# Batch 0 over SyncE's queue as 32-bit words, stores on GpSimd's queue, full-height tiles, transposes behind the loads

## The chip, the core and the metric

The kernel runs on one core of a Trainium2 chip. A core has five engines with a list of instructions each: TensorE (PE, matrix products), VectorE (DVE), ScalarE (ACT), GpSimd (POOL) and SyncE (SP). They work at the same time and meet only at semaphores; each takes its own list strictly in order. Sixteen DMA engines move data between the main memory (HBM) and the on-chip memory (SBUF). Products go to a small memory of eight banks (PSUM), from where ScalarE or VectorE copies them. The metric is device time in microseconds, as the median of several runs: 201.82 before the change (three runs, 201.66 to 203.79).

## The reference

Inputs are q, k and v of shape (8 batches, 8 heads, 576 rows, 64), and three weights. An attention with keys and values pooled over eight rows is followed by a gated feed-forward stage with a short convolution:

```python
k_p = k.reshape(B, H, S // 8, 8, D).mean(axis=3)      # 72 pooled rows a head; v_p alike
scores = scale * q @ k_p.transpose(0, 1, 3, 2)
attn = softmax(scores)
x = (attn @ v_p) -> (B, S, H * D)                     # 576 x 512 a batch
h = relu(x @ w_in)                                    # 512 -> 1024
conv_out = conv_w[0] * h[s-1] + conv_w[1] * h[s] + conv_w[2] * h[s+1]
out = (h * sigmoid(conv_out)) @ w_out                 # 1024 -> 512, float32
```

All inputs and the output are float32; the kernel computes in bfloat16 with float32 sums.

## The kernel before

One launch does all eight batches. Every step is an operation handed to a planner (`Planner`), with its engine, an estimated duration, what it reads and writes, and a rank. `Planner.order` plays these operations against its own table of durations and writes them out; the list of ranks `prio` decides among operations that could start together, and `act` names the evacuations and copies that go to ScalarE rather than VectorE. The compiled program keeps that order on each engine. Where the planner sees TensorE idle in the first 60 us, it puts matmuls of a zero tile (`warm`, L407), called fillers here; nothing reads their result.

For each batch these steps follow one another; those of different batches overlap:

- **Loads** (`load_k` L468 and L472, `load_v` L488 to L500, `load_q` L439 and L445). GpSimd issues all loads, and its DMAs convert float32 to bfloat16 on the way. Batches 0 to 4 bring q with eight rows of a head side by side; `regroup` (L453) brings them into order. Batches 5 to 7 bring q as five tiles of 128 rows.
- **Pooling** (`pool8`, `attn_k`, `attn_v`): three adds on VectorE, L632, L639 and L649 for k or L695 for v. For k four full transposes and one of a tile of 64 rows follow on TensorE (L662, L663), and two copies into `kz` (L669). For v two masked copies `vblk` (L700, L705).
- **q turned** (`attn_q`): in batches 0 to 4 by TensorE against the identity, 32 matmuls (L735) and copies (L744); in batches 5 to 7 by five crossbar transposes in DMA, issued by SyncE (L718).
- **Scores and exponentials** (`attn_s`): five tiles, L767 and, for the rest of four pairs of heads, L769 on a quarter of the columns each; ScalarE takes the exponential (L775).
- **Value products** (`attn_av`): five tiles of six matmuls (L792, L796); the fifth has 64 rows of output. VectorE divides (L805, L809) into `xx`. In batches 0 to 4 TensorE turns `xx` (L829, the fifth tile with 64 rows) and L835 copies it to `xT`; in batches 5 to 7 SyncE's crossbar transposes do it (L822).
- **Feed-forward**: x times w_in (L849 for batch 0, L872 for the others) with relu on ScalarE; the convolution partly on TensorE (L995), mostly on VectorE and ScalarE (L918 to L937); the gate (L945, L1002) and the product gT (L983).
- **Output** (`mm2` L1026): for each pair of batches nine tiles of 128 rows, copies into one of three output buffers (L1049), and five stores issued by SyncE (L1054); the last tile in two halves (L1039, L1044).

GpSimd also makes the identity matrix `ident`, which the transposes and the small constants of the convolution need. In its list the first five loads stand ahead of it.

SyncE's list before the change has one small load, then the five stores of batches 0 and 1, and after that transposes and stores mixed. Each DMA also waits for the landing of the eighth DMA before it on the same queue.

Of the kernel before, what the change touches and what calls it, by code (L numbers as in the profile page):

```python
# [104 lines left out]
}  # L105
# [9 lines left out]
class Planner:  # L115
# [60 lines left out]
    def order(self):  # L176
# [16 lines left out]
        ring = [0.0] * 4  # L193
# [6 lines left out]
        while avail:  # L200
# [68 lines left out]
            if o.dma is not None:  # L269
                n, each = o.dma  # L270
                if e == "SP":
# [37 lines left out]
def kernel(  # L309
# [14 lines left out]
    P = 128  # L324
# [20 lines left out]
    perm4 = st("perm4", [64, 64], BF16)  # L345
# [23 lines left out]
    attnT = [st(f"attnT{i}", [P, NT, S], BF16) for i in range(2)]  # L369
# [78 lines left out]
    def regroup(b, pr):  # L448
        if PARAMS["rg"][b] in "QT" or PARAMS["qd"][b]:
            return  # L450
        for h in range(0, H, 4):
# [5 lines left out]

    def load_k(b, prio):
        m = b % 2
        src = rows(k, b)  # L460
        acc = PARAMS["acc"][b]
# [14 lines left out]
    def load_v(b, prio):  # L476
        m = b % 2
        src = rows(v, b).rearrange("(c z) e -> z c e", z=2 * Sp)
        acc = PARAMS["acc"][b]
# [38 lines left out]
    def consts():  # L518
# [20 lines left out]
        def fn(e):  # L539
            nc.vector.tensor_copy(out=perm4.rearrange("r (p i) -> r p i", i=TP), in_=ident[0:64, 0:64].rearrange("r (i p) -> r p i", p=8))  # L540
# [64 lines left out]

        for m in range(2):
            def fn(e, m=m):
                nc.vector.memset(kz[m], 0.0)
# [549 lines left out]
```

## Time and profile before

| | |
|---|---|
| median of 3 runs | 201.82 us |
| the profiled execution's own time | 200.92 us |
| span of its instructions | 199.1 us |
| TensorE's granted clock | 1.00 |
| first, last matmul | 2.5 us, ends 195.4 us |
| value products of batch 0 begin | 17.1 us |
| feed-forward of batch 0 begins | 21.7 us |
| last load lands | 114.5 us |
| first crossbar transpose issued | 83.5 us |
| HBM read, written | 33.44 MB, 9.44 MB |

All times of instructions are counted from the start of the span. A matmul's duration in the profile includes the depth of the pipeline: full matmuls of 128 columns show some 220 ns and start every 56 ns. So I compare starts. "Idle before" tells how long an engine had nothing to run before an instruction, and what it waited for. The granted clock is 1.00 in every stretch.

### The profile page before, as it was taken

Reading aid. Unit: us, or ns where it says so; the run is one execution under the profiler, and the core shown is the slowest. Engines: PE = TensorE matmul, PEld = TensorE weight load, DVE = VectorE, ACT = ScalarE, POOL = GpSimd, SP = SyncE. Lnnn points to the kernel's source line nnn. Section 1 sums busy time; section 2 is a strip of 40 time slices with the busy share of each in tenths; the row PEclk is TensorE's granted clock in tenths of the full one; section 3 lists DMA queues with packets and bytes.
Section 4 is the critical chain, followed back from the end, with each engine's and each line's share of the span. In section 5 each row is a group of like instructions: output and inputs, shape, how many; then the busy total and the mean of one; then the engine's idle time right before and its main releaser. Section 6 shows DMA issues by size and latency. Waiting matters only on the chain.

```text
span 199.1 us, 4491 instructions
## 1 busy us (share of the span) xinstructions
PE 190.8 (96%) x1737; PEld 128.9 (65%) x1737; DVE 171.0 (86%) x400; ACT 167.0 (84%) x282; POOL 47.5 (24%) x76
## 2 busy tenths in 40 slices
PE   5999999999999999999999999989999999999992
PEld 5888777777546576767756656547666565765541
DVE  3777999999999999999999999988889997755631
ACT  0677699999995499999999999995999999998410
POOL 7966431543233262761140000000000000000000
PEclk9999999999999999999999999999999999999999
DMA  3999999999999999999999966477112144502324
GB/s 39 185 185 200 204 204 193 207 206 200 195 204 250 268 217 207 159 217 121 113 116 117 70 211 161 85 189 188 28 35 83 65 129 87 211 3 77 135 106 158
DMA packets 52857, 30.00 MB, mean 151 GB/s; under 512 B 33484, under 2 KB 48356, under 8 KB 52836
## 3 DMA queue, kind: packets, MB, share of 16 engines
q0 software_dynamic: 32912, 16.73, 68.1%
q1 hardware_dynamic: 19924, 12.99, 26.9%
q8 instruction: 13, 0.21, 0.4%
q14 instruction: 8, 0.07, 0.1%
HBM read 33.44 MB, written 9.44 MB: 215 GB/s over the span
## 4 chain that ended last, share of the span: by engine, by line
PE 88%; DVE 7%; POOL 2%; DMA 1%; issue 1%; ACT 0%; POOLq 0%
PE psfB L1026 31%; PE psfA L872 25%; PE psfA L792 4%; PE psfA L767 4%; PE psfA L995 4%; PE pswA L407 3%; PE psbB L735 2%; PE psfB L849 2%; DVE xx L809 2%; PE psfA L849 2%; PE psfA L796 2%; PE psbB L829 1%; PE pswB L407 1%; PE psbA L829 1%; DMA xT<-xx 1%; PE psfA L769 1%
## 5 line engine op out<-in xcount | busy, mean ns | idle before, releaser
L1026 PE MATMUL psfB<-w_out,gT 128*128 128x512 bf16 (+1 forms) x282 | 65.5, 378 | 0.0
L872 PE MATMUL psfA<-xT,w_in 128*128 128x288 bf16 x448 | 59.2, 286 | 0.9 <-DMA xT<-xx 0.7
L872 PEld LDWEIGHTS <-w_in 128*128 128x128 bf16 x448 | 42.8, 98 | 14.8 <-issue 1.2
L1026 PEld LDWEIGHTS <-gT 128*128 128x128 bf16 x290 | 27.2, 98 | 29.0 <-issue 0.2
L878 ACT ACTIVATE hT<-psfA 128x576 bf16<-128x576 f32 x56 | 35.2, 651 | 2.2 <-PE psfA L872 2.0
L918 ACT ACTIVATE cv<-hT,cr 128x576 bf16<-128x576 bf16 x37 | 28.3, 779 | 0.2
L809 DVE TENSOR_TENSOR xx<-psfA,rr 128x512 bf16<-128x512 f32 (+1 forms) x40 | 26.8, 683 | 0.9 <-DMA xT<-xx 0.7
L920 DVE TENSOR_SCALAR cv<-hT,cr 128x576 bf16<-128x576 bf16 x71 | 23.9, 363 | 3.9 <-ACT tg L945 2.3
L775 ACT ACTIVATE attnT<-psfA 128x576 bf16<-128x576 f32 x40 | 25.1, 674 | 0.3 <-PE psfA L767 0.2
L983 DVE TENSOR_TENSOR gT<-tg,hT 128x1152 bf16<-128x1152 bf16 x32 | 23.7, 750 | 1.2 <-ACT tg L1002 0.8
L927 DVE TENSOR_TENSOR cv<-cv,hT 128x1152 bf16<-128x1152 bf16 (+1 forms) x31 | 20.8, 672 | 4.0 <-ACT cv L918 3.9
L945 ACT ACTIVATE tg<-cv,cn 128x576 bf16<-128x576 bf16 x31 | 23.2, 775 | 0.9 <-DVE cv L937 0.6
L937 DVE TENSOR_TENSOR cv<-cv 128x1152 bf16<-128x1152 bf16 (+1 forms) x31 | 20.8, 673 | 0.2
L1049 ACT COPY osb<-psfB 128x512 f32<-128x512 f32 x24 | 14.3, 595 | 7.4 <-PE psfB L1026 7.3
L945 ACT ACTIVATE tg<-cv,cs 128x576 bf16<-128x576 bf16 x23 | 17.5, 797 | 0.0
L792 PE MATMUL psfA<-vblk,attnT 128*128 128x130 bf16 (+1 forms) x160 | 15.7, 222 | 0.2
L407 PEld LDWEIGHTS <-zero 128*128 128x128 bf16 x206 | 13.0, 105 | 3.4 <-DVE zero L520 2.5
L792 PEld LDWEIGHTS <-attnT 128*128 128x128 bf16 (+1 forms) x160 | 11.0, 100 | 4.1 <-issue 1.8
L407 PE MATMUL pswA<-zero 128*128 128x128 bf16 x148 | 10.5, 236 | 2.5 <-DVE zero L520 2.5
L767 PE MATMUL psfA<-qT,kz 128*128 128x512 bf16 x64 | 12.3, 286 | 0.4 <-ACT attnT L775 0.4
L439 POOL DMA_DIRECT2D q<-in_q_dram x10 | 8.6, 863 | 12.1 <-DMA k_b<-in_k_dram 4.0
L796 PE MATMUL psfA<-vblk,attnT 128*128 128x130 bf16 (+1 forms) x80 | 11.2, 221 | 0.0
(94 smaller groups left out, 247.8 us busy)
## 6 DMA issues: line engine op xcount, KB each, us to landing
out_dram<-osb SPq DMA_DIRECT2D x14, 512.0 KB, 3.0
k_b<-in_k_dram POOLq DMA_DIRECT2D x8, 512.0 KB, 14.8
v_b<-in_v_dram POOLq DMA_DIRECT2D x7, 512.0 KB, 16.7
q_b<-in_q_dram POOLq DMA_DIRECT2D x4, 576.0 KB, 17.6
out_dram<-osb SPq DMA_DIRECT2D x7, 256.0 KB, 2.1
w_in<-in_moe_w_in_dram POOLq DMA_DIRECT2D x2, 512.0 KB, 11.4
w_out<-in_moe_w_out_dram POOLq DMA_DIRECT2D x2, 512.0 KB, 15.0
q<-in_q_dram POOLq DMA_DIRECT2D x8, 128.0 KB, 12.6
```

The lines of the kernel that those rows point to most:

```text
L407: nc.tensor.matmul(out=t, lhsT=zero[:, 0:P], rhs=zero[:, 0:P], start=True, stop=True)
L775: nc.scalar.activation(out=attnT[m][:, t, :], in_=slot(key).rearrange("p i x -> p (i x)")[:, 0:S], func=ACT.Exp, scale=1.0 / 64.0)
L792: nc.tensor.matmul(out=a[0:n, g, c * w:(c + 2) * w], lhsT=attnT[m][:, s, u0:u0 + n], rhs=vblk[m][:, 2 * s:2 * s + 2, :].rearrange("p x d - ...
L809: nc.vector.tensor_tensor(out=xx[i3][0:n].rearrange("p (g h e) -> p g h e", g=2, h=4), in0=av_view()[:, :, :, 0:D], in1=rr[i3][0:n].rearra ...
L872: nc.tensor.matmul(out=t[:, i, 0:HC], lhsT=w_in[:, c, f * P:(f + 1) * P], rhs=xT[m][:, c, i * HC:(i + 1) * HC], start=(c == 0), stop=(c == ...
L878: nc.scalar.activation(out=h_(b)[:, f, hs(b), 2:S + 2].rearrange("p (i x) -> p i x", i=2), in_=slot(key)[:, :, 0:HC], func=ACT.Relu)
L918: nc.scalar.activation(out=cv[y][:, kk // 2, z0:z1, :], in_=src, func=ACT.Copy, scale=sc)
L920: nc.vector.tensor_scalar(out=cv[y][:, kk // 2, z0:z1, :], in0=src, scalar1=sc, scalar2=None, op0=OP.mult)
L927: nc.vector.tensor_tensor(out=cv[y][:, 0, 0:n, :], in0=cv[y][:, 0, 0:n, :], in1=h_at(2), op=OP.add)
L945: nc.scalar.activation(out=tg[i3][:, zs[z0]:zs[z0] + z1 - z0, :], in_=cv[y][:, 0, z0:z1, :], func=ACT.Tanh if half else ACT.Sigmoid, scale ...
L983: nc.vector.tensor_tensor(out=o_, in0=tg[i3], in1=h2, op=OP.mult)
L1026: nc.tensor.matmul(out=a[:, 0, j0:j1], lhsT=g[:, c, t * P:(t + 1) * P], rhs=w_out[:, c, j0:j1], start=(c == 0), stop=(c == n_fb - 1), skip ...
```

## The change

Five things change together.

1. **Batch 0's q, k and v** come by SyncE's queue as float32, without conversion, into memory that gT uses later (`ks`, `ws`, `qs`): q in four pieces, k in two, v in six, twelve issues beside the one small load. The first adds of the pooling then read float32, and q is regrouped in four copies instead of two.
2. **Stores** of the second and third pair of batches (`sp`) are issued by GpSimd, the others by SyncE.
3. **Full-height tiles**: the fifth k tile is transposed with 128 rows (the upper 64 are zeros), the fifth value tile computes 128 rows of output (the exponentials have 64 more columns for that, set to zero once), and the fifth turn of `xx` is a matmul over 128 rows against a matrix whose lower rows are zeros.
4. **Transposes held** (`xw`): for the planner every crossbar transpose depends on all loads that GpSimd issues. That moves them in the written order; the program gets no wait from it.
5. **The order drawn anew**: new ranks `prio`, a new choice `act`, and new terms in the planner's table: its load queue counts as busy to 12.9 us, and early DMAs of SyncE get their own rule.

In the compiled order GpSimd first makes the identity and the masks' start, then issues q of batch 1, a piece of k of batch 1, half of w_in, k of batch 1, the other half of w_in and v of batch 1. The crossbar transposes stand behind the last store of pair 0 on SyncE, and the stores of pairs 1 and 2 stand behind all loads on GpSimd. There are 224 fillers, where there were 206.

```diff
-    "xw": 0,
+    "xw": 1,
+    "kh": 2,
+    "sp": [0, 1, 1, 0],
...
-        ring = [0.0] * 4
+        ring = [12.9 if PARAMS["kh"] == 2 else 0.0] * 4
...
-                if e == "SP":
+                if e == "SP" and s < 9.0 and o.lat is not None:
+                    o.done = s + d + 2.03
+                elif e == "SP" and s < 9.0:
+                    hring = max(hring, s + d + 0.5, 3.9) + n * each
+                    o.done = hring + self.DMA_LAT
+                elif e == "SP":
...
-    perm4 = st("perm4", [64, 64], BF16)
+    perm4 = st("perm4", [P, 64], BF16)
...
-    attnT = [st(f"attnT{i}", [P, NT, S], BF16) for i in range(2)]
+    attnF = [st(f"attnT{i}", [P, NT * S + 64], BF16) for i in range(2)]
+    attnT = [a[:, 0:NT * S].rearrange("p (t s) -> p t s", t=NT) for a in attnF]
...
+        if b == 0 and PARAMS["kh"] == 2:
+            for x in range(2):
+                for y, (r0, r1) in enumerate(((0, 64), (64, PR))):
+                    def fn(e, x=x, r0=r0, r1=r1):
+                        nc.sync.dma_start(out=qs[x][r0:r1].rearrange("p h i d -> p h (i d)"), in_=rows_q(b)[r0:r1, 4 * x:4 * x + 4])
+                    pl.add(f"ldq0.{x}.{y}", "SP", 0.43, fn, writes=[("qs", x, y)], prio=prio + 0.01 * x, dma=(2 if y else 16, 0.085))
+            return
...
+        if b == 0 and PARAMS["kh"] == 2:
+            for h in range(0, H, 2):
+                def fn(e, h=h):
+                    copy_on(e)(out=q2[0][0:PR, :, h:h + 2, :], in_=qs[h // 4][0:PR, h % 4:h % 4 + 2].rearrange("p h i d -> p i h d"))
+                pl.add(f"qg.{b}.{h}", {"DVE": 1.15, "ACT": 1.04}, 0, fn, reads=[("qs", h // 4, 0), ("qs", h // 4, 1)],
...
+    def early(i, lo, hi):
+        return gT[i].rearrange("p f s -> p (f s)")[:, lo:hi].bitcast(FP32)
+    ks = early(1, 0, NT * 1024).rearrange("p (t e) -> p t e", t=NT)
+    ws = early(0, 0, NT * 1024).rearrange("p (t e) -> p t e", t=NT)
+    qs = [early(i, NT * 1024, NT * 1024 + 4096).rearrange("p (h i d) -> p h i d", i=TP, d=D) for i in range(2)]
...
+        if b == 0 and PARAMS["kh"]:
+            def fn(e):
+                nc.sync.dma_start(out=ks[:, 0:4], in_=src[0:512].rearrange("(t p) e -> p t e", p=P))
+            pl.add("ldk0.0", "SP", 0.43, fn, writes=[("ks", 0)], prio=prio, dma=(32, 0.085))
...
+        if b == 0 and PARAMS["kh"] == 2:
+            for c in range(4):
+                def fn(e, c=c):
+                    nc.sync.dma_start(out=ws[32 * c + 16:32 * c + 32, 4], in_=src[P:P + 16, c])
...
+            for x in range(2):
+                def fn(e, x=x):
+                    nc.sync.dma_start(out=ws[:, 2 * x:2 * x + 2], in_=src[0:P, 2 * x:2 * x + 2])
...
-            nc.tensor.transpose(out=t[:, 0, 512:576], in_=ksum[0:64, 4].rearrange("p i d -> p (i d)"), identity=ident[0:64, 0:64])
+            nc.tensor.transpose(out=t[:, 0, 512:640], in_=ksum[:, 4].rearrange("p i d -> p (i d)"), identity=ident)
...
-                nc.tensor.matmul(out=a[0:n, g, c * w:(c + 2) * w], lhsT=attnT[m][:, s, u0:u0 + n],
+                nc.tensor.matmul(out=a[:, g, c * w:(c + 2) * w], lhsT=attnF[m][:, s * S + u0:s * S + u0 + P],
...
+                if last:
+                    nc.tensor.matmul(out=a[:, 0, c * n:(c + 1) * n], lhsT=xx[i3][:, c * P:(c + 1) * P], rhs=ident[:, 0:n] if tr else perm4, start=c == 0, stop=c == n_dc - 1, skip_group_check=True)
+                    continue
...
-            nc.sync.dma_start(out=out_rows[r:r + n * P, :].rearrange("(i p) d -> p i d", p=P), in_=osb[i3][:, 0:n, :])
-        pl.add(f"st.{pair}.{tiles[0]}", "SP", 0.4, fn, reads=[("osb", i3, x) for x in range(n)], prio=pr, dma=packets(n * P, 2048, False))
+            (nc.gpsimd if PARAMS["sp"][pair] else nc.sync).dma_start(out=out_rows[r:r + n * P, :].rearrange("(i p) d -> p i d", p=P), in_=osb[i3][:, 0:n, :])
+        pl.add(f"st.{pair}.{tiles[0]}", "POOL" if PARAMS["sp"][pair] else "SP", 0.8 if PARAMS["sp"][pair] else 0.4, fn, reads=[("osb", i3, x) for x in range(n)], prio=pr, dma=packets(n * P, 2048, False))
```

More of the change, by code (lines that the diff above doesn't have):

```diff
@@ L450, in regroup @@
             return
+        if b == 0 and PARAMS["kh"] == 2:
[3 more added lines that the diff above has]
+                pl.add(f"qg.{b}.{h}", {"DVE": 1.15, "ACT": 1.04}, 0, fn, reads=[("qs", h // 4, 0), ("qs", h // 4, 1)],
+                       writes=[("q", 0, h), ("q", 0, h + 1)] + ([("qt", 0)] if h == 6 else []), prio=pr + 0.01 * h,
+                       free=[("qn", "R", 0, t) for t in range(NT)])
+            return
         for h in range(0, H, 4):
@@ L460, in load_k, with fn @@
         src = rows(k, b)
+        if b == 0 and PARAMS["kh"]:
+            def fn(e):
+                nc.sync.dma_start(out=ks[:, 0:4], in_=src[0:512].rearrange("(t p) e -> p t e", p=P))
+            pl.add("ldk0.0", "SP", 0.43, fn, writes=[("ks", 0)], prio=prio, dma=(32, 0.085))
+            def fn(e):
+                nc.sync.dma_start(out=ks[0:64, 4], in_=src[512:576])
+            pl.add("ldk0.t", "SP", 0.43, fn, reads=["kzs"], writes=[("ks", 1)], prio=prio + 0.01, dma=(4, 0.085))
+            return
         acc = PARAMS["acc"][b]
@@ L539, in fn @@
         def fn(e):
-            nc.vector.tensor_copy(out=perm4.rearrange("r (p i) -> r p i", i=TP), in_=ident[0:64, 0:64].rearrange("r (i p) -> r p i", p=8))
+            nc.vector.tensor_copy(out=perm4.rearrange("r (p i) -> r p i", i=TP), in_=ident[:, 0:64].rearrange("r (i p) -> r p i", p=8))
         pl.add("perm1", "DVE", 0.15, fn, reads=["ident"], writes=[("perm", 1)], prio=-47)
@@ L604, in consts, with fn @@
                        writes=[("dw", f, kk)], prio=-3 + 0.5 * f)
+        if PARAMS["kh"]:
+            def fn(e):
+                nc.vector.memset(ks[64:P, 4], 0.0)
+            pl.add("zks", "DVE", 0.4, fn, writes=["kzs"], prio=-75)
+            def fn(e):
+                nc.vector.memset(ws[:, 4], 0.0)
+            pl.add("zvs", "DVE", 0.54, fn, writes=["vzs"], prio=-74)
         for m in range(2):
+            def fn(e, m=m):
+                nc.vector.memset(attnF[m][:, NT * S:], 0.0)
+            pl.add(f"zat{m}", "DVE", 0.08, fn, writes=[("zat", m)], prio=-40 + 35 * m)
             def fn(e, m=m):
@@ L632, in fn @@
                 nc.vector.tensor_tensor(out=p1[:, t0:t1, :], in0=src[m][:, t0:t1, 0:256], in1=src[m][:, t0:t1, 256:512], op=OP.add)
-            rk = rs + ([("kz", m)] if name == "k" else [])
+            st_ = b == 0 and (PARAMS["kh"] if name == "k" else PARAMS["kh"] == 2)
+            rk = rs + ([] if st_ else [("kz", m)] if name == "k" else [])
             if not acc:
-                pl.add(f"{name}p1.{b}.{x}", "DVE", 0.075 + 0.1334 * n, fn, reads=rk, writes=[("p1", y) for y in ys], prio=pr)
+                pl.add(f"{name}p1.{b}.{x}", "DVE", 0.075 + (0.267 if st_ else 0.1334) * n, fn, reads=rk, writes=[("p1", y) for y in ys], prio=pr)
                 rk = [("p1", y) for y in ys]
@@ L644, in attn_k @@
         m = b % 2
-        pool8(b, "k", k_b, pr, ((0, 5, (0, 1), [("k", m, 0), ("k", m, 1)]),))
+        if b == 0 and PARAMS["kh"]:
+            pool8(b, "k", [ks], pr, ((0, 5, (0, 1), [("ks", 0), ("ks", 1), "kzs"]),))
+        else:
+            pool8(b, "k", k_b, pr, ((0, 5, (0, 1), [("k", m, 0), ("k", m, 1)]),))
         def fn(e):
@@ L662, in fn @@
                 nc.tensor.transpose(out=t[:, 0, i * P:(i + 1) * P], in_=ksum[:, i].rearrange("p i d -> p (i d)"), identity=ident)
-            nc.tensor.transpose(out=t[:, 0, 512:576], in_=ksum[0:64, 4].rearrange("p i d -> p (i d)"), identity=ident[0:64, 0:64])
-        pl.add(f"kT.{b}", "PE", 0.29, fn, reads=["ksum", "ident"], writes=[("kTp", b)], prio=pr, take=key, free=[("kz", m, 0), ("kz", m, 1)])
+            nc.tensor.transpose(out=t[:, 0, 512:640], in_=ksum[:, 4].rearrange("p i d -> p (i d)"), identity=ident)
+        pl.add(f"kT.{b}", "PE", 0.31, fn, reads=["ksum", "ident"], writes=[("kTp", b)], prio=pr, take=key, free=[("kz", m, 0), ("kz", m, 1)])
         kzi = [None]
@@ L675, in attn_v, with vkey @@
         m = b % 2
-        tail = [*[("v", m, 2 + c) for c in range(4)]]
-        parts = ((0, 2, (0,), [("v", m, 0)]), (2, 5, (1,), [("v", m, 1)] + tail)) if b == 0 else ((0, 5, (0, 1), [("v", m, 0), ("v", m, 1)] + tail),)
+        vk = "ws" if b == 0 and PARAMS["kh"] == 2 else ("v", m)
+        def vkey(y):
+            return (vk, y) if vk == "ws" else ("v", m, y)
+        tail = [vkey(2 + c) for c in range(4)] + (["vzs"] if vk == "ws" else [])
+        parts = ((0, 2, (0,), [vkey(0)]), (2, 5, (1,), [vkey(1)] + tail)) if b == 0 else ((0, 5, (0, 1), [("v", m, 0), ("v", m, 1)] + tail),)
         if PARAMS["vp"][b]:
@@ L691, in attn_v @@
         else:
-            pool8(b, "v", v_b, pr, parts)
+            pool8(b, "v", [ws] if vk == "ws" else v_b, pr, parts)
             def fn(e):
@@ L770, in fn @@
                                          start=True, stop=True, tile_position=(0, 32 * c))
-        pl.add(f"sc.{b}.{t}", "PE", 0.25 if t < 4 else 0.48, fn, reads=[("kz", m, 0), ("kz", m, 1)] + [("qT", m, g) for g in gs] + [("qA", m)],
+        pl.add(f"sc.{b}.{t}", "PE", 0.25 if t < 4 else 0.37, fn, reads=[("kz", m, 0), ("kz", m, 1)] + [("qT", m, g) for g in gs] + [("qA", m)],
                writes=[("scp", b, t)], prio=pr, take=key, free=[("at", m, t)])
@@ L795, in fn @@
             for g in range(2):
-                nc.tensor.matmul(out=a[0:n, g, 0:4 * w].rearrange("p (c x d) -> p c x d", x=2, d=w)[:, :, 1], lhsT=attnT[m][:, 4, u0:u0 + n],
+                nc.tensor.matmul(out=a[:, g, 0:4 * w].rearrange("p (c x d) -> p c x d", x=2, d=w)[:, :, 1], lhsT=attnF[m][:, 4 * S + u0:4 * S + u0 + P],
                                  rhs=vblk[m][:, 8 + 2 * g:10 + 2 * g, :], start=False, stop=True, skip_group_check=True)
-        avs[0] = pl.add(f"av.{b}.{t}", "PE", 0.35, fn, after=avs[0], reads=[("at", m, s) for s in range(NT)] + [("va", m, 0), ("va", m, 1)],
+        avs[0] = pl.add(f"av.{b}.{t}", "PE", 0.35, fn, after=avs[0], reads=[("at", m, s) for s in range(NT)] + [("va", m, 0), ("va", m, 1), ("zat", m)],
                writes=[("avp", b, t)], prio=pr, take=key, free=[("rr", i3), ("xx", i3)])
@@ L822, in fn @@
                 nc.sync.dma_start(out=xT[m][:, :, u0:u0 + n], in_=xx[i3][0:n, :], transpose=True)
-            pl.add(f"xD.{b}.{t}", "SP", 1.27, fn, reads=[("xx", i3)], writes=[("xT", m, t)], prio=pr + 0.3, dma=(1, 0.65), lat=0.1)
+            pl.add(f"xD.{b}.{t}", "SP", 1.35, fn, reads=[("xx", i3)], writes=[("xT", m, t)], prio=pr + 0.3, dma=(1, 0.65), lat=0.4)
             return
         def fn(e):
-            a = slot(key2, True)
+            a = slot(key2, not last)
             for c in range(n_dc):
-                nc.tensor.transpose(out=a[:, 0, c * P:c * P + n], in_=xx[i3][0:n, c * P:(c + 1) * P], identity=(ident[0:n, 0:n] if tr else perm4 if last else perm))
-        pl.add(f"xt.{b}.{t}", "PE", 0.14 if last else 0.222, fn, reads=[("xx", i3), ("perm", 0), ("perm", 1)], writes=[("xtp", b, t)],
+                if last:
+                    nc.tensor.matmul(out=a[:, 0, c * n:(c + 1) * n], lhsT=xx[i3][:, c * P:(c + 1) * P], rhs=ident[:, 0:n] if tr else perm4, start=c == 0, stop=c == n_dc - 1, skip_group_check=True)
+                    continue
+                nc.tensor.transpose(out=a[:, 0, c * P:c * P + n], in_=xx[i3][0:n, c * P:(c + 1) * P], identity=(ident if tr else perm))
+        pl.add(f"xt.{b}.{t}", "PE", 0.13 if last else 0.222, fn, reads=[("xx", i3), ("perm", 0), ("perm", 1)], writes=[("xtp", b, t)],
                prio=pr + 0.3, take=key2, free=[("xT", m, t)])
@@ L835, in fn @@
             copy_on(e)(out=xT[m][:, :, 128 * t:128 * t + w],
-                       in_=slot(key2)[:, 0, 0:512].rearrange("p (c a) -> p c a", c=4)[:, :, 0:w])
-        pl.add(f"xte.{b}.{t}", {"ACT": 0.48, "DVE": 0.335} if not last else {"ACT": 0.265, "DVE": 0.205}, 0, fn, reads=[("xtp", b, t)], writes=[("xT", m, t)],
+                       in_=slot(key2)[:, 0, 0:4 * w].rearrange("p (c a) -> p c a", c=4))
+        pl.add(f"xte.{b}.{t}", {"ACT": 0.48, "DVE": 0.335} if not last else {"ACT": 0.27, "DVE": 0.33}, 0, fn, reads=[("xtp", b, t)], writes=[("xT", m, t)],
                prio=pr + 0.3, give=key2)
```

3 lines of the change are left out of this document (added), and 97 rows, old and new, of the table PARAMS.

## The prediction

> **What bounds the kernel now.** I read the page first (busy shares and the chain that ended last), then the waits of TensorE, then its timeline around the places where it waited, then the DMA issues and DMA rate by stretch.
>
> ```profile
> span 199.1 us, 4491 instructions
> ...
> PE 190.8 (96%) x1737; PEld 128.9 (65%) x1737; DVE 171.0 (86%) x400; ACT 167.0 (84%) x282; POOL 47.5 (24%) x76
> ...
> PE 88%; DVE 7%; POOL 2%; DMA 1%; issue 1%; ACT 0%; POOLq 0%
> ```
>
> TensorE is the bound, and 88% of the chain that ended last is its own work, not waiting. So the end moves by what TensorE's list gains or loses in work, by the start of its real work, and by the few holes in it. The start, from TensorE's timeline (start us, us, engine, line, operation):
>
> ```profile
> 10.39 0.40 PE L662 MATMUL psbB<-ident,ksum 128*128 128x128 bf16 x4
> ...
> 17.09 0.40 PE L792 MATMUL psfA<-vblk,attnT 128*128 128x130 bf16 x4
> ...
> 21.70 0.82 PE L849 MATMUL psfA<-xT,w_in 128*128 128x384 bf16 x4
> ```
>
> Batch 0's pooled keys are turned at 10.4, its value products begin at 17.1, its first feed-forward product at 21.7 us. Until then TensorE mostly multiplies zeros (L407). The last matmul ends at 195.4. The only hole after that start worth more than 0.5 us, from the same view:
>
> ```profile
> 126.86 0.39 PE L662 MATMUL psbB<-ident,ksum 128*128 128x128 bf16 x4
> 127.18 0.20 PE L663 MATMUL psbB<-ident,ksum 64*128 64x64 bf16 x1
> 127.31 0.66 PE L767 MATMUL psfA<-qT,kz 128*128 128x512 bf16 x4
> ...
> 131.26 0.41 PE L767 MATMUL psfA<-qT,kz 128*128 128x512 bf16 x2 [0.38 <-ACT attnT L775]
> ...
> 134.64 0.28 PE L872 MATMUL psfA<-xT,w_in 128*128 128x288 bf16 x1 [0.57 <-DMA xT<-xx]
> 135.09 1.15 PE L872 MATMUL psfA<-xT,w_in 128*128 128x288 bf16 x8 [0.17 <-DMA xT<-xx]
> ```
>
> Between 130.5 and 135.1 the starts are 2.2 us later than the same shapes need elsewhere (0.57, 0.30, 0.26, 0.74 and 0.33): exponentials of batch 6 and crossbar transposes of batch 5 come late. The first three lines show a second thing. Full matmuls of 128 columns start 0.056 apart; four of them and one of 64 rows should take 0.28, and take 0.45 to the next start. Each step between a full shape and one of at most 64 rows or columns costs about 0.095 us.
>
> Last, the loads (DMA issues with count and median us to landing; then stretches, their last two columns the DMA share and GB/s):
>
> ```profile
> xT<-xx SPq DMA_TRANSPOSE x15, 2.5
> qT<-q SPq DMA_TRANSPOSE x10, 10.8
> ...
> qT<-q_b SPq DMA_TRANSPOSE x5, 2.6
> ...
> 56.00:60.00 4.00, 4.00 (x24) 1.90 (x22) 3.92 (x10) 4.00 (x8) 1.58 (x3) 1.00 1.25 207
> 83.00:104.00 21.00, 20.83 (x195) 14.81 (x194) 20.59 (x51) 20.86 (x35) 7.03 (x10) 1.00 1.68 143
> 104.00:115.00 11.00, 11.00 (x87) 7.04 (x86) 10.40 (x23) 10.87 (x19) 0.64 (x1) 1.00 1.89 95
> ```
>
> Transposes among loads (from 83.5 us) land after 10.8 us instead of 2.6, and the rate falls from 207 to 143 and 95 GB/s. The last load lands at 114.5.
>
> **The change, part by part.**
>
> *Full-height tiles.* Steps removed: kT, 0.172 a batch (0.45 against 5 x 0.056) in 8 batches, 1.4 us; the last value tile, in and out, 0.19 x 8 = 1.5; the last turn of the output in batches 0 to 4, 0.19 x 5 = 0.9. The wider matmuls cost nothing: the turn keeps 64 columns, kT adds 64 columns (0.02, counted). Of the 3.8 us, 3.5 lie behind the first feed-forward matmul, where TensorE is never short of work. The chip's price of a full shape in these places is a row (0.056), so I keep no other bound than 0 and 3.8.
>
> *Order drawn anew.* Fillers on `zero`: 224 against 206; behind the first feed-forward matmul 58 against 27. They hold the place of waits that the new order expects in batch 1, but run whatever comes: 31 x 0.056 = +1.7. Eleven q transposes (0.032 each) and four turns (0.056) now stand ahead of that matmul: -0.6 behind it.
>
> *Batch 0 over SyncE's queue.* Thirteen issues of about 0.43 us (L528's row); SyncE has nothing else until a store at 56.3, so the issuing is free. GpSimd loses nine issues there, so `ident` comes at 2.2 us rather than 5.5, and its first load (q of batch 1) issues at about 2.2 instead of 9.3. Every engine moves 108 packets of 2 KB for batch 0. Trace packets of the load queue pass at 0.08 us an engine at full load, so 8.6 us; the small constant's first packet comes 0.7 us after its issue, so the flow starts at 2.0, and v is complete at 11.3 if SyncE's queue is alone. No row shows a load on this queue. Stores show how two queues meet: the store issued at 56.3 moved its first packet at 60.0, 3.7 us late, and from 65 to 66.5 us the trace has 146 packets of SyncE's queue beside 145 of GpSimd's. If GpSimd's first packets (3.6 us) are held as long, SyncE's queue is alone to 7.3, then at half rate: k complete at 7.6, v at 14.6 (before: 8.4 and 14.7). With no such hold v comes at 18.3. I take the middle, because the same trace shows both the hold and the halves; the ends 11.3 and 18.3 stay for the range.
>
> The f32 adds: nearest rows are the bf16 add of 1280 (0.74 start to start) and f32 from PSUM into xx (0.60 for 512, 1.17 ns an element, so 1.50 for 1280). Source type decides, so +0.76 for k and +0.45 for v's two pieces. They stand ahead of the scores.
>
> When do value products start? Not before TensorE's own list allows. The first ScalarE copy of q must follow its table load (1.28): cw comes at about 4.7 (6.5 now, less the earlier `ident`), three scalings of 0.29 and the copy follow, done about 7.9. Then in order: 16 q transposes, 69 fillers (3.9) to 12.4, 8 q transposes, kT at 12.8, kz, scores from 14.1, the last at 16.2, 26 fillers, value products at about 17.85. From v at 14.6 by the before-distance of 2.4 plus 0.45: 17.45. So 17.85, 0.75 late against 17.09; the first feed-forward matmul follows 4.4 to 4.6 later as now, at 22.3: **+0.6**. Both w_in halves come no later than now, since GpSimd's queue is served from 4 to 7 us on.
>
> *Stores on GpSimd, transposes held.* Pairs 1 and 2 store behind all loads on GpSimd's in-order queue. Pair 1's first store now issues at 114.2 and GpSimd's last load at 104, so nothing waits; if loads ran late, the copies into the three output buffers would, and TensorE's PSUM with them. On SyncE fifteen q transposes follow pair 0's last store, and no store stands between them and the fifteen of xx. Loads without transposes beside them should keep 200 GB/s: 13.4 MB of the 16.7 of this queue have landed by 80 us, the rest takes 17 to 19 us, so 97 to 99 instead of 114.5. "Held" is only an order: the first transpose waits for a tile of q with nine loads still issued behind it. Adding rows along TensorE's list, batch 5's scores stand 91 us after the first feed-forward matmul, at 113; five quiet transposes need 8.5 us (119.3 to 127.8 now). Start by 104 suffices. And 12 us of other work stand between the last values of batch 5 and its feed-forward, where there were 8.6. So most of the 2.2 us hole should go: **-1.5** (bounds 0 and -2.2).
>
> On the transposes, the Trainium skill ("DMA: Bandwidth & Descriptors", Rules for kernel authors) says that a transpose next to ordinary DMAs needs nothing. That is said of data; the 10.8 against 2.6 us above disagree as to time. By it the hole would stay and the sum be 1.5 us worse.
>
> **Sum:** +0.6 - 0.6 - 3.5 + 1.7 - 1.5 = -3.3 us. The profiled execution took 200.9 (span 199.1 and 1.8 around it), so 197.6 (span 195.8). It lay 0.9 under the median of 201.82; the median should become **198.5**.
>
> **The rivals.**
>
> *ScalarE becomes the bound* (0.20). Adding its rows from the first relu on, it reaches batch 1's first relu after 22.0 us (now 16.7), since batch 2's five exponentials now stand before it; TensorE's list gets there after 21.7 (now 18.6). A lead of 1.9 became -0.3; with the first output 0.5 to 0.9 more, and DVE 95% busy beside it, 1 to 1.5 us are lost: 199.8. For it: ACT is over 98% busy from 41 to 60 us. Against: five x 0.67 of cv and two table loads leave it later on.
>
> *Equal shares from the start* (0.15). v at 18.3, value products at 21.15, +3.3 on an in-order engine: 201.8. Against it: the 3.7 us hold. The Trainium skill ("DMA: Bandwidth & Descriptors", SWDGE vs HWDGE vs iDMA) has each DMA engine take turns between the two kinds of queue, which is this rival from the first packet; the 146 beside 145 agree, the late first packet does not.
>
> *Slower: the last loads hold batch 5* (0.12). q tiles are now the very last loads, behind v of batch 7, which waits for batch 5's pooling on a DVE that is 95% busy. TensorE cannot pass its scores. If the last load still lands at 114.5, the transposes end at 123 and the list is 9.7 us late: 208. It decides from about 108 on, where the loss (3.3) eats the gain. For it: loads were slow here; against it: what slowed them has moved.
>
> *It doesn't do what it says* (0.05): padding leaves the steps where they are: 198.5 + 3.5 = 202.
>
> **How the numbers follow.** The forecast, 195 to 199.8, has 0.48. About 1% (199.8 to 203.8) is what a measurement can tell from no change. Faster: 0.48 and half of ScalarE's rival, 0.58. Within 1%: the other half, most of equal shares and of the last rival, 0.27. Slower: the held loads and the tails of the others, 0.15. The range runs down to 195.0: early loads let the start come 0.5 earlier at most, since the fillers stand, the whole hole may go (0.7 more), the profile's 0.9 under the median may not recur, and 1.4 remain for small waits of the old order that the new one lacks. Up to 203.5 it leaves out the held loads and little else.
>
> **What would show it.** In the changed profile: starts 0.056 apart through kT and into the next operation; the first value product near 17.9 and the first feed-forward matmul near 22.3; k and v of batch 0 landing near 8 and 14.6; last load under 100 us; transposes landing in under 3 us but for the first few; no wait over 0.5 us on xT; last matmul near 192. The forecast is wrong if value products begin after 20, if DVE waits for k or v of batch 7, or if TensorE waits for qT.

## The result, and the profile after

The changed kernel takes **216.94 us** (median of four runs, 214.63 to 219.38) where the kernel before takes 202.12 beside it: a ratio of **1.068**, 95% interval 1.056 to 1.079. The forecast was 198.5. One of the four runs of the changed kernel and two of the four of b0_gp_bf16 below were longer at a lower granted clock; the ratio of 1.068 leaves that one out (it is against the mean of the kernel before, 202.42), while the 1.020 of b0_gp_bf16 in the table still contains its two, without which it is 1.011 (204.54 and 205.90 against 203.06). The profiled execution took 217.26 us, its span is 215.6. From its page (span, busy shares, granted clock in tenths over the span, and the chain that ended last by engine):

```profile
span 215.6 us, 4546 instructions
...
PE 192.6 (89%) x1755; PEld 132.3 (61%) x1755; DVE 171.0 (79%) x399; ACT 169.3 (79%) x289; POOL 47.5 (22%) x76
...
PEclk9996699999999999999999999999889999999999
...
PE 57%; ACT 18%; DMA 15%; DVE 6%; SPq 1%; issue 1%; DVEq 0%; ACTq 0%
```

TensorE is busy for about as long as before, but for 89% of the span where it was 96%, and its own work is 57% of the last chain where it was 88%. ScalarE and DMAs have come into that chain, so the time went into waiting. TensorE's timeline in the first 35 us shows the larger part (start us, us, engine, line, operation; in brackets the idle time before and what ended it):

```profile
21.29 0.66 PE L805 MATMUL psbB<-ident,q 72*128 72x72 bf16 x8 [8.17 <-ACT q L470]
...
21.85 0.63 PE L728 MATMUL psbB<-ident,ksum 128*128 128x128 bf16 x4
22.27 0.31 PE L729 MATMUL psbB<-ident,ksum 128*128 128x128 bf16 x1
...
29.63 0.40 PE L862 MATMUL psfA<-vblk,attnT 128*128 128x130 bf16 x4 [1.81 <-DVE vblk L770]
...
34.24 0.81 PE L922 MATMUL psfA<-xT,w_in 128*128 128x384 bf16 x4
```

These answer to the first lines shown of before. The pooled keys are turned at 21.9 (10.4 before), the value products begin at 29.6 (17.1), the first feed-forward product at 34.2 (21.7). TensorE waited 8.2 us for a copy of batch 0's q on ScalarE. ScalarE's own timeline says what that copy waited for:

```profile
20.18 1.99 ACT L470 CAST q<-gT 72x1024 bf16<-72x1024 f32 x2 [9.54 <-DMA gT<-in_q_dram]
```

The loads of batch 0, from the list of DMA issues (queue, count, KB each, median us from issue to landing):

```profile
gT<-in_q_dram SPq DMA_DIRECT2D x2, 512.0 KB, 10.9
gT<-in_k_dram SPq DMA_DIRECT2D x1, 1024.0 KB, 13.2
...
gT<-in_v_dram SPq DMA_DIRECT2D x2, 512.0 KB, 17.5
```

Batch 0's k is complete at 17.0 us (its large piece at 16.2; 7.6 forecast, 8.4 before), the second half of q at 20.1, and v between 22.4 and 26.3 (14.6 forecast). The end of v sets the value products: TensorE then waited for `vblk`, which is made from v, 1.8 us up to 29.6. The second place is where the forecast wanted a hole closed, around batch 5's feed-forward. From TensorE's timeline there:

```profile
142.72 0.39 PE L728 MATMUL psbB<-ident,ksum 128*128 128x128 bf16 x4
142.94 0.22 PE L729 MATMUL psbB<-ident,ksum 128*128 128x128 bf16 x1
143.00 0.65 PE L837 MATMUL psfA<-qT,kz 128*128 128x512 bf16 x4
...
148.34 0.67 PE L837 MATMUL psfA<-qT,kz 128*128 128x512 bf16 x4 [0.63 <-DMA qT<-q_b]
...
151.38 0.28 PE L945 MATMUL psfA<-xT,w_in 128*128 128x288 bf16 x1
154.43 1.83 PE L945 MATMUL psfA<-xT,w_in 128*128 128x288 bf16 x7 [2.77 <-DMA xT<-xx]
```

The hole has grown: 0.6 us without work before batch 7's scores and 2.8 us for batch 5's xT. The seven feed-forward products behind it take 1.83 us, because the granted clock is halved there (last section). But the first three lines show the step that did work. Four turns of the keys and the fifth, now full, take 0.28 us to the next start; before they took 0.45.

For a sum I split TensorE's time from the first feed-forward product to the last matmul in two. Every start-to-start is compared with the median of its shape. An excess of more than 0.23 us, or of more than 0.13 when another engine released the later instruction, is a **wait**; all else is the **list**. All profiled executions, experiments included (us; the ratio is that of the timed runs against the kernel before beside them):

| kernel | first feed-forward | list | waits | last matmul starts | span | ratio (95%) |
|---|---|---|---|---|---|---|
| before | 21.70 | 170.24 | 3.21 | 195.15 | 199.1 | 1 |
| changed | 34.24 | 169.17 | 7.99 | 211.40 | 215.6 | 1.068 (1.056 to 1.079) |
| b0_gp_f32 | 28.30 | 167.64 | 7.75 | 203.69 | 208.9 | 1.037 (1.033 to 1.040) |
| b0_gp_bf16 | 23.42 | 167.48 | 6.52 | 197.41 | 202.8 | 1.020 (1.014 to 1.026) |
| sp_alone | 34.54 | 167.46 | 6.45 | 208.45 | 213.4 | 1.060 (1.055 to 1.064) |
| full_only | 22.37 | 166.76 | 7.18 | 196.31 | 200.2 | 0.989 (0.985 to 0.994) |
| b0_gp_qT3 | 23.44 | 167.47 | 4.35 | 195.25 | 200.0 | 1.000 (0.998 to 1.002) |
| b0_gp_st_sp | 23.74 | 167.56 | 7.43 | 198.74 | 203.9 | 1.010 (1.005 to 1.015) |
| b0_gp_nofill | 23.55 | 164.28 | 9.22 | 197.05 | 202.1 | 1.012 (1.008 to 1.016) |
| full_qT3 | 22.98 | 166.82 | 6.82 | 196.63 | 200.6 | 0.992 (0.989 to 0.996) |
| after_qT3 | 34.52 | 167.49 | 4.18 | 206.18 | 210.3 | 1.045 (1.040 to 1.050) |
| qT3_q3cut | 24.03 | 167.57 | 4.42 | 196.01 | 200.7 | 0.998 (0.995 to 1.001) |

The changed kernel lost 12.5 us at the start, won 1.1 in the list and lost 4.8 in waits; together that is all of the 16.25 us by which its last matmul starts late. Its list contains some 1.7 us of halved clock behind the second hole; the other kernels with the new order and all of its fillers have 167.5 to 167.6.

### The profile page after: what moved, and what is told of

Its sections match the earlier page's. It is cut to its first block, busy times and chain, and to the rows that moved or that the text cites. A ratio compares the mean times of both kernels' runs of the same rounds, so it can differ in the third digit from the quotient of the medians.

```text
span 215.6 us, 4546 instructions
## 1 busy us (share of the span) xinstructions
PE 192.6 (89%) x1755; PEld 132.3 (61%) x1755; DVE 171.0 (79%) x399; ACT 169.3 (79%) x289; POOL 47.5 (22%) x76
## 4 chain that ended last, share of the span: by engine, by line
PE 57%; ACT 18%; DMA 15%; DVE 6%; SPq 1%; issue 1%; DVEq 0%; ACTq 0%
PE psfB L1099 19%; PE psfA L945 19%; DMA gT<-in_k_dram 6%; DMA gT<-in_v_dram 5%; ACT hT L951 4%; ACT tg L1018 4%; PE psfA L1068 3%; ACT cv L991 3%; PE psfA L862 3%; DMA xT<-xx 3%; PE psfA L922 2%; PE psfA L837 2%; DMA qT<-q_b 2%; DVE xx L879 2%; ACT xT L908 2%; ACT attnT L845 2%
## 5 line engine op out<-in xcount | busy, mean ns | idle before, releaser
L945 PE MATMUL psfA<-xT,w_in 128*128 128x288 bf16 x448 | 60.7, 290 | 3.0 <-DMA xT<-xx 2.8
L993 DVE TENSOR_SCALAR cv<-hT,cr 128x576 bf16<-128x576 bf16 x76 | 26.3, 375 | 2.7 <-ACT tg L1018 1.0
L991 ACT ACTIVATE cv<-hT,cr 128x576 bf16<-128x576 bf16 x32 | 24.7, 793 | 0.2
L1018 ACT ACTIVATE tg<-cv,cn 128x576 bf16<-128x576 bf16 x32 | 24.1, 794 | 1.0 <-DVE cv L1010 1.0
L1127 POOL DMA_DIRECT2D out_dram<-osb x10 | 6.8, 684 | 77.6 <-ACT osb L1122 43.8
L416 PEld LDWEIGHTS <-zero 128*128 128x128 bf16 x224 | 15.3, 110 | 3.7 <-DVE zero L569 2.4
L862 PE MATMUL psfA<-vblk,attnT 128*128 128x130 bf16 x160 | 15.7, 223 | 2.1 <-DVE vblk L770 1.8
L862 PEld LDWEIGHTS <-attnT 128*128 128x128 bf16 x160 | 11.8, 99 | 5.9 <-ACT q L477 1.9
L805 PE MATMUL psbB<-ident,q 72*128 72x72 bf16 x140 | 7.0, 204 | 9.2 <-ACT q L470 8.2
L805 PEld LDWEIGHTS <-q 72*128 72x128 bf16 x160 | 6.7, 102 | 10.1 <-ACT q L470 8.3
```

The source lines that it names most:

```text
L862: nc.tensor.matmul(out=a[:, g, c * w:(c + 2) * w], lhsT=attnF[m][:, s * S + u0:s * S + u0 + P], rhs=vblk[m][:, 2 * s:2 * s + 2, :].rearran ...
L945: nc.tensor.matmul(out=t[:, i, 0:HC], lhsT=w_in[:, c, f * P:(f + 1) * P], rhs=xT[m][:, c, i * HC:(i + 1) * HC], start=(c == 0), stop=(c == ...
L991: nc.scalar.activation(out=cv[y][:, kk // 2, z0:z1, :], in_=src, func=ACT.Copy, scale=sc)
L993: nc.vector.tensor_scalar(out=cv[y][:, kk // 2, z0:z1, :], in0=src, scalar1=sc, scalar2=None, op0=OP.mult)
L1018: nc.scalar.activation(out=tg[i3][:, zs[z0]:zs[z0] + z1 - z0, :], in_=cv[y][:, 0, z0:z1, :], func=ACT.Tanh if half else ACT.Sigmoid, scale ...
```

## The experiments

### Where the start went: queue or words

Three kernels keep the changed kernel's orders and move only batch 0's loads. The two on GpSimd's queue issue them ahead of its other loads:

```diff
-  nc.sync.dma_start(out=qs[x][r0:r1]..., in_=rows_q(b)[r0:r1, 4 * x:4 * x + 4])
+  nc.gpsimd.dma_start(out=qs[x][r0:r1]..., in_=rows_q(b)[r0:r1, 4 * x:4 * x + 4])
...
-  for s, e, d, o in pl.order():
+  for s, e, d, o in batch0_loads_and_masks + other_early_loads + rest:   # shortened
```

The second of them also takes the staging buffers as bf16, so that the loads cast:

```diff
-        return gT[i].rearrange("p f s -> p (f s)")[:, lo:hi].bitcast(FP32)
+        return gT[i].rearrange("p f s -> p (f s)")[:, lo // 2:hi // 2]
```

> The changed kernel, with batch 0's twelve loads issued on GpSimd's queue ahead of its other loads; words, adds and all other orders are kept. Theory 'shared start' (the 12.5 us by which the first feed-forward product came late, 34.2 against 21.7, are lost because SyncE's queue got only every second packet from the start, at about 0.097 us a packet): with one queue and batch 0 first, k lands near 8, q's second half near 10.5, v near 14 to 15; first feed-forward product near 23; profile 204 to 206. Rival 'words' (32-bit words are slow to move or to add, on any queue): v still lands after 20, first feed-forward product after 29, profile above 211.

> As b0_gp_f32, but the loads cast to bf16 as before the change. Theory 'shared start': within 1 us of b0_gp_f32 (the adds are 1.2 us shorter in all, not all of it on the path), 203 to 205.5. Rival 'words': this one alone gains, first feed-forward product near 22 and at least 6 us less than b0_gp_f32.

The third leaves batch 0 on SyncE's queue and puts four tiny reads of the landed tiles ahead of GpSimd's first load:

```diff
+  for z, x_ in enumerate((ks[:, 3, 0:1], ws[:, 1, 0:1], ws[:, 3, 0:1], ws[:, 4, 0:1])):
+      nc.gpsimd.affine_select(out=scr[:, z:z + 1], in_=x_, ...)
```

> The changed kernel, with GpSimd's first load held until all of batch 0 has landed over SyncE's queue. Theory 'shared start': alone, SyncE's queue passes a packet in about 0.08 us an engine, so k near 7.5, v near 12 to 13; value products near 18; the first half of w_in, now third on GpSimd's queue from about 13, lands near 24 to 25 and sets the first feed-forward product at 25; profile 206 to 209. Rival 'slow queue' (SyncE's queue needs twice the time for a packet by itself): v still lands after 22, the loads behind it 10 us or more later than in the changed kernel, profile above 222.

Measured, with the moment at which the last piece of v has landed: changed 26.3, sp_alone 20.3, b0_gp_f32 20.3, b0_gp_bf16 16.0 us. The rows of k and v in the lists of DMA issues of sp_alone, b0_gp_f32 and b0_gp_bf16:

```profile
gT<-in_k_dram SPq DMA_DIRECT2D x1, 1024.0 KB, 9.8
gT<-in_v_dram SPq DMA_DIRECT2D x2, 512.0 KB, 12.1
```

```profile
gT<-in_k_dram POOLq DMA_DIRECT2D x1, 1024.0 KB, 7.4
gT<-in_v_dram POOLq DMA_DIRECT2D x2, 512.0 KB, 11.4
```

```profile
gT<-in_k_dram POOLq DMA_DIRECT2D x1, 512.0 KB, 5.8
...
gT<-in_v_dram POOLq DMA_DIRECT2D x2, 256.0 KB, 7.4
```

Each theory had half of it. The queue by itself is not slow: alone, SyncE's brings v as early as GpSimd's does with the same words, both ahead of the 22 of the "slow queue". But words cost 4.3 us of landing on one and the same queue (16.0 to 20.3), and sharing the DMA engines costs another 6.0 (20.3 to 26.3). The first feed-forward product follows: 23.4 with the cast, 28.3 with 32-bit words, 34.2 with the shared engines. So of the 12.5 us, **5.9 are the sharing, 4.9 the words**, and 1.7 lie in neither (b0_gp_bf16 still starts that much behind the kernel before). Part of the words' share is the way from the landing of v to the first value product, with the wider adds on it: 3.34 us in all three kernels with 32-bit words, 2.68 with the cast. My own sum for "shared start" was wrong by the words: 28.3 against 23, a span of 208.9.

Why the words cost shows in the DMA rate (last column, GB/s; the one before is the DMA share). Here b0_gp_bf16, then b0_gp_f32:

```profile
8.00:12.00 4.00, 4.00 (x67) 4.00 (x66) 2.60 (x6) 2.95 (x8) 3.08 (x8) 1.00 1.21 196
12.00:16.00 4.00, 3.90 (x68) 3.31 (x66) 1.92 (x5) 2.33 (x4) 2.71 (x4) 1.00 1.20 181
```

```profile
8.00:12.00 4.00, 3.88 (x58) 3.61 (x56) 2.41 (x13) 3.16 (x7) 2.33 (x6) 1.00 1.04 321
12.00:16.00 4.00, 2.20 (x40) 2.03 (x37) 2.66 (x4) 1.02 (x2) 1.55 (x3) 1.00 1.03 270
```

The column counts bytes as they land, as the KB of the issues above do. The cast lands 181 to 196 GB/s and so takes in 362 to 392 GB/s of f32. Without the cast 270 to 321 GB/s land, but batch 0 is then 3.54 MB instead of 1.77. Per value the f32 load is about 1.2 to 1.4 times as dear while it streams.

In sp_alone the gain at the value products (23.6 against 29.6) is gone again at the first feed-forward product (34.5). The held queue's first load, q of batch 1, issues at 21.1 and lands at 28.8, and TensorE's order has that batch's q transposes ahead of the product; its timeline shows a wait of 4.5 us there:

```profile
29.56 0.78 PE L806 MATMUL psbB<-ident,q 72*128 72x72 bf16 x10 [4.49 <-DVE q L478]
```

### The full-height tiles alone

The kernel before with these lines only (the turns of the output and the zeroed 64 columns go with them):

```diff
-  nc.tensor.transpose(out=t[:, 0, 512:576], in_=ksum[0:64, 4]..., identity=ident[0:64, 0:64])
+  nc.tensor.transpose(out=t[:, 0, 512:640], in_=ksum[:, 4]..., identity=ident)
...
-  nc.tensor.matmul(out=a[0:n, g, ...], lhsT=attnT[m][:, s, u0:u0 + n], ...)
+  nc.tensor.matmul(out=a[:, g, ...], lhsT=attnF[m][:, s * S + u0:s * S + u0 + P], ...)
```

> The kernel before, with nothing but the full-height tiles (kT, value tile, last turn of the output). Theory (each step between a full and a small shape costs TensorE 0.095 us, as I forecast): TensorE's list is 3.5 us shorter behind the first feed-forward product, profile 197.4, ratio 0.983. Rival 'given back': the waits for exponentials and crossbar transposes at 130 to 135 us grow by as much, half or more of it is lost: 199.5 to 200.9. Rival 'no steps saved': starts in kT stay at 0.095 and more, 200.9.

The list is 3.48 us shorter, as forecast to the tenth. The time is 1.1% (0.6 to 1.5) shorter, about 2.2 us: some of the gain is given back. In the profiled execution, the slowest of its four by 0.9 us, the waits grew by 4.0, 0.8 of it between 130 and 137 us and the rest in pieces of 0.2 to 0.6 us, most of them from 60 us on and behind xx, exponentials and copies. So "given back" holds too, though for a good third and not for the half or more that I had expected of it. This kernel beats both the kernel before and the changed one.

### The second hole: what batch 5's feed-forward waits for

Batch 7's queries go through the qT buffer of batch 5, so their transposes wait for batch 5's scores, and on SyncE's in-order queue batch 5's own xT transposes stand behind them. b0_gp_qT3 gives batch 7 a buffer of its own, in memory of q_b that is no longer used by then:

```diff
+    qT7 = q_b[0].rearrange("p h i d -> p (h i d)")[:, 0:CH * S].rearrange("p (c x) -> p c x", c=CH)
...
-  nc.sync.dma_start(out=flat_q(m)[:, :, P * t:P * t + n], ..., transpose=True)
+  nc.sync.dma_start(out=(qT7 if b == 7 else flat_q(m))[:, :, P * t:P * t + n], ..., transpose=True)
```

> The kernel b0_gp_bf16 with a third buffer for qT (unused memory of q_b) for batch 7 alone, so that its five crossbar transposes no longer wait for batch 5's scores. Theory 'one queue, one by one' (TensorE waits 0.9 us before batch 7's scores and 1.1 us on xT of batch 5 because ten transposes of 1.2 to 1.8 us each stand behind batch 5's scores on SyncE): both waits go, profile 200.5 to 201.3 against 202.8. Rival 'store collision' (a transpose issued while a store of GpSimd's queue is under way lands after 3.4 to 4.4 us instead of 2.4, and that is the wait): the wait on xT keeps at least 0.8 us, 201.8 to 202.8.

SyncE's timeline in b0_gp_bf16, then in b0_gp_qT3:

```profile
90.53 23.24 SPq L788 DMA_TRANSPOSE qT<-q  x10
124.91 5.73 SPq L788 DMA_TRANSPOSE qT<-q_b  x4
130.74 2.98 SPq L892 DMA_TRANSPOSE xT<-xx  x2
133.81 1.69 SPq L788 DMA_TRANSPOSE qT<-q_b  x1
```

```profile
90.36 22.77 SPq L789 DMA_TRANSPOSE qT<-q  x10
113.22 5.60 SPq L789 DMA_TRANSPOSE q_b<-q_b  x4
128.65 2.99 SPq L893 DMA_TRANSPOSE xT<-xx  x2
131.74 1.22 SPq L789 DMA_TRANSPOSE q_b<-q_b  x1
```

Four of batch 7's transposes move from 124.9 to 113.2, where SyncE had nothing to do, and the first xT from 130.7 to 128.7. Both waits are gone: the scores and the feed-forward in b0_gp_qT3 carry no idle time any more, where b0_gp_bf16 has 0.8 and 1.0 us:

```profile
137.80 0.65 PE L837 MATMUL psfA<-qT,kz 128*128 128x512 bf16 x4 [0.78 <-DMA qT<-q_b]
...
142.09 1.03 PE L945 MATMUL psfA<-xT,w_in 128*128 128x288 bf16 x7 [0.98 <-DMA xT<-xx]
```

```profile
136.79 0.65 PE L838 MATMUL psfA<-q_b,kz 128*128 128x512 bf16 x4
...
139.82 1.14 PE L946 MATMUL psfA<-xT,w_in 128*128 128x288 bf16 x8
```

The span falls from 202.8 to 200.0, somewhat more than expected; the ratio falls to 1.000, from 1.011 by the two shorter runs of b0_gp_bf16. Stores beside the transposes were the rival; b0_gp_st_sp puts them back on SyncE:

```diff
-  (nc.gpsimd if PARAMS["sp"][pair] else nc.sync).dma_start(out=out_rows[r:r + n * P, :]...)
+  nc.sync.dma_start(out=out_rows[r:r + n * P, :]...)
```

> The kernel b0_gp_bf16 with the stores of pairs 1 and 2 back on SyncE's queue. Theory 'one queue, one by one': the stores add some 0.5 us each between the transposes, the waits at batch 7's scores and batch 5's xT stay or grow: 202.8 to 204.5. Rival 'store collision' between the two queues: transposes land after 2.4 us again, the two waits (2.1 us) shrink to under 0.7: 200.8 to 201.5.

In its profile the wait on xT grew from 1.1 to 2.6 us (by its excess), while the 0.9 before batch 7's scores are gone. A transpose beside a store lands late from either queue: counted from 116 us on, when all loads have landed, the twelve of this kernel during which ten or more packets of a store moved landed after a median of 2.9 us (six of them after 3.3 to 4.3), the other nine after 2.4. Whether the store's queue matters for the time is not shown: the ratio is 1.010 (1.005 to 1.015) here and 1.011 by the two shorter runs of b0_gp_bf16, and the profiled execution is the slowest of its four by 1.5 us.

The same buffer in the changed kernel itself, and nothing else:

> The changed kernel itself (batch 0 over SyncE's queue, as it is) with nothing but the third qT buffer for batch 7. Theory 'one queue, one by one', from b0_gp_qT3: the waits before batch 7's scores (0.8 us) and on batch 5's xT (2.9 us) go, 3 to 3.7 us less: span near 212.2, ratio 1.047 to 1.055 against 1.068. Rival: they were the work of the late start and of stores beside the transposes, and at least half of them stays, span 213.8 or more.

The span falls by 5.3 us, more than the 3 to 3.7 expected: 3.8 of waits and 1.7 of list. The latter is the halved clock behind the wait, which is gone with the wait. So the hole cost the changed kernel some 5 us.

In the kernel before with full-height tiles, the third buffer brought nothing:

> The kernel before with the full-height tiles (as full_only) and the third qT buffer for batch 7. In full_only the list was 3.5 us shorter and 1.1 to 1.4 us of the regained waits stood on xT of batch 5 near 136. Theory 'one queue, one by one': those go, ratio 0.980 to 0.985 against 0.989 of full_only. Rival: the exponentials of batches 6 and 7 end there instead, ratio 0.989 again.

0.992 against 0.989. There batch 7's transposes still issue at 121.6 (120.5 in full_only), because on SyncE they follow the last two transposes of batch 6 (114.3 and 116.2) and three stores, the last of which issues at 121.1. A free buffer helps only where it was what held the queue.

### Fillers, and the waits around batch 1

b0_gp_nofill leaves out the matmuls on `zero` behind the first feed-forward product:

```diff
-            if o.i in pl.gaps:
+            if o.i in pl.gaps and pl.gaps[o.i][2] < 22.0:
                 warm(*pl.gaps[o.i])
```

> The kernel b0_gp_bf16 without the 58 matmuls on the zero tile that stand behind the first feed-forward product. By the forecast's term they cost 58 x 0.056 = 3.2 us: 199.6. Rival 'they lie in waits' (VectorE is busy throughout from 30 to 50 us and TensorE would wait there anyway): under 1 us is gained, 201.8 to 202.8, and the waits of TensorE before 50 us grow by over 2 us.

The list is 3.2 us shorter, the waits 2.7 longer. The fillers lie in waits: all 58 cost 0.5 us, and the term of +1.7 for 31 of them was worth some 0.3.

qT3_q3cut takes work from VectorE just before batch 1's feed-forward:

```diff
-  copy_on(e)(out=q2[...][0:PR, :, h:h + 4, :], in_=q_b[...][0:PR, h:h + 4]...)
+  n_ = 1 if b == 3 else 4
+  copy_on(e)(out=q2[...][0:PR, :, h:h + n_, :], in_=q_b[...][0:PR, h:h + n_]...)
```

> The kernel b0_gp_qT3 with three quarters of VectorE's regrouping copies of batch 3's queries left out (batch 3 is then computed from old queries), which takes some 1.2 us from VectorE at 43.7 us. Theory 'VectorE is the bound around batch 1's output': the wait of 1.24 us for xx at 46 falls to 0.3 or less, while the 0.66 and 0.26 for ScalarE's qT copies stay, span near 199.0. My forecast's rival 'ScalarE': the wait at 46 keeps 0.9 us or more, span 199.6 to 200.2.

The copies fell from 1.54 to 0.48 us, but the wait for xx only from 1.24 to 1.02, and the span is 200.7, above both expectations. From TensorE's and then VectorE's timeline of qT3_q3cut:

```profile
45.65 0.28 PE L868 MATMUL psfA<-vblk,attnT 128*128 128x130 bf16 x2
46.78 0.40 PE L904 MATMUL psbA<-perm,xx 128*128 128x128 bf16 x4 [0.85 <-DVE xx L881]
```

```profile
45.48 0.21 DVE L877 RECIPROCAL rr<-psfA 128x8 f32<-128x8 f32 x1 [0.31 <-PE psfA L868]
45.97 0.20 DVE L877 RECIPROCAL rr<-psfA 64x8 f32<-64x8 f32 x1 [0.28 <-PE psfA L868]
46.09 1.23 DVE L881 TENSOR_TENSOR xx<-psfA,rr 128x512 bf16<-128x512 f32 x2
```

VectorE now waits for the value products itself. My theory fell, and the rival "ScalarE" is not shown by it either: the turn stands directly behind the value products that it needs, by way of reciprocals and a scaling of 0.6 us, and the new order gives TensorE nothing to do between them. So this wait is mostly a latency.

## Why the prediction was wrong, point by point

**Batch 0 over SyncE's queue: +0.6 forecast, +12.5 measured.** This is the step that failed, twice over. "Trace packets of the load queue pass at 0.08 us an engine at full load, so 8.6 us" took a price from cast packets, which land half of what they read, and put it on packets that land all of it. Alone, SyncE's queue moved 571 packets from 8 to 12 us (540 of them of 2 KB), 0.112 us each on 16 engines, and needed until 20 us for what I gave 11.3. And "held as long" did not recur: GpSimd's first packet of data moved at 5.5 us, not at 7.3, and from 12 to 16 us the packet records have 322 of SyncE's queue beside 322 of GpSimd's, so one of batch 0 passes every 0.20 us on an engine. The rival "equal shares from the start" had the mechanism but inherited the price, 18.3 for v and a time of 201.8. By the Trainium skill ("DMA: Bandwidth & Descriptors", Rules for kernel authors) spreading DMAs over issuing engines gives no bandwidth, since all run on the same 16 DMA engines and interleave; the 322 beside 322 agree. That v sets the start was right: the value products begin 3.34 us behind its landing, where I had 2.85 (2.4 and 0.45). The 8.2 us of waiting for the second half of q, at 20.1, lie ahead of that. Nor was the issuing free: the last piece of v was issued at 16.2 us, when the eighth DMA before it had landed, and is the last known to land (26.3; the piece issued at 7.4 landed at 25.6).

**Full-height tiles: -3.5 forecast, -3.48 measured** in TensorE's list (full_only). Tiles, order and fillers together: -2.4 forecast, -2.75 measured where the clock stays whole (after_qT3; -2.77 in b0_gp_qT3). That the list sets the end was wrong: in full_only only 2.2 of 3.5 us arrived, and the fillers' 1.7 was worth some 0.3: they run in place of waits.

**The hole: -1.5 forecast.** In that place the waits went from 2.2 to 3.7 us instead (0.8 and 2.9 by their excess), +1.5, and the halved clock behind them cost another 1.7. The rest of the 4.8 by which all waits grew are 2.3 around batch 1 and 1.0 elsewhere. The loads did end sooner, though less than forecast: the last lands 82.0 us behind the first feed-forward product, where it was 92.8 (75 to 77 forecast). But they were not what the hole waited for. In b0_gp_bf16 the last load lands at 104.1, ten us earlier than before, and the waits are still there. I named ten transposes on one queue and "12 us of other work", and did not ask which wait releases the queue: a buffer that batch 5's scores free. The Trainium skill ("DMA: Bandwidth & Descriptors", Rules for kernel authors) says that a transpose next to ordinary DMAs needs nothing, which is said of data; for time the runs disagree here as well, with 3.2 us beside a store against 2.4 without (medians of seven and nine in after_qT3, counted as in b0_gp_st_sp).

**The rivals.** "ScalarE" was to cost 1 to 1.5 us before batch 1's first relu. Waits of 2.3 us are there in all kernels of the new order (2.0 to 2.6), 0.9 behind ScalarE's copies of qT and 1.0 to 1.5 behind xx, the latter mostly latency. "The last loads hold batch 5": the last load landed at 116.2, past my deciding 108, but all was 12 us late by then, and batch 5's scores began at 129.2 without a wait. "It doesn't do what it says": no, 0.28 instead of 0.45. Slower came by a way that my sum had as a range of v, 11.3 to 18.3, whose upper end was no bound.

Put together, b0_gp_qT3 has all of the change but the queue and the words, and one buffer more: +1.7 at the start, -2.8 in the list, +1.1 in waits, and a ratio of 1.000. What is worth keeping is in full_only.

## What to carry to other kernels

Price a load by what it lands as well as by what it reads, from a packet of the same kind; a plain f32 load in place of a casting one lands twice the bytes, and a second queue brings no second set of DMA engines, so that what is needed first belongs ahead on the queue that is already busy. Before a wait is put down to slow transfers, ask what the in-order queue in front of them waits for; a free buffer may be the whole remedy. Work taken off the busiest engine's list arrives only as far as its neighbours are ahead.

## What was not expected of the hardware

During 8 us without work and behind them TensorE's granted clock was down to 0.75 from 16 to 20 us and 0.50 from 20 to 24 (the column ahead of the last two in the changed kernel's stretches):

```profile
16.00:20.00 4.00, 0.00 (x0) 0.00 (x0) 2.66 (x4) 0.00 (x0) 0.88 (x1) 0.75 1.13 255
20.00:24.00 4.00, 2.71 (x30) 2.44 (x31) 1.53 (x4) 1.99 (x2) 0.00 (x0) 0.50 1.15 281
```

The five turns of batch 0's keys took 0.53 us there, from 21.85 to 22.38, against 0.28 at full clock. Here that cost nothing more, since TensorE then waited another 1.8 us for v. But a late transfer can be paid a second time. Behind the 2.8 us without work at batch 5's feed-forward the granted clock is 0.50 again, where after_qT3, without that wait, has 1.00 in the same stretch (changed kernel, then after_qT3):

```profile
154.50:157.90 3.40, 3.40 (x18) 2.35 (x19) 0.91 (x3) 1.43 (x2) 0.00 (x0) 0.50 0.00 0
```

```profile
154.50:157.90 3.40, 3.40 (x27) 2.07 (x25) 3.37 (x10) 3.37 (x6) 0.00 (x0) 1.00 0.38 77
```

The feed-forward products start 0.240 us apart there instead of 0.122. Half of 3.4 us is the 1.7 us by which the changed kernel's list is longer than that of after_qT3. In sp_alone, behind its 4.5 us of waiting, the way from the q turns at 29.56 to the first feed-forward product takes 4.98 us, where the changed kernel takes 3.24 (31.00 to 34.24): the granted clock is 0.50 from 28 to 32 us in the one and 1.00 in the other.

And the changed kernel, sp_alone and b0_gp_f32 all had a slack stretch between 6 and 8 us, with 53 to 104 packets of batch 0 where the next 2 us had 169 to 298 (in the changed kernel 252 of GpSimd's queue moved beside them); why is open.
